# Second layers in another order of tiles, difference parts and raw second-layer weights at other steps

## The chip, the cores and the metric

The kernel runs on one core of one Trainium2 chip. Its time is the device time of the whole program in microseconds (us). A trace of one execution is told in its own time, from the first instruction on (the span).

## What is computed

Two parts follow each other. The first is a gated linear recurrence over 768 positions, for 4 sequences and 8 heads of width 48. The second sends its output, 3072 rows of 384, through four experts, each of two layers with a ReLU between, and adds the results weighted by a probability.

```python
# recurrence: q, k, v, alpha are (4, 8, 768, 48)
for t in range(S):
    state = alpha[:, :, t, :, None] * state + np.einsum('bhd,bhe->bhde', k[:, :, t], v[:, :, t])
    y[:, :, t] = np.einsum('bhd,bhde->bhe', q[:, :, t], state)
x = y.transpose(0, 2, 1, 3).reshape(B * S, H * D)          # (3072, 384)
# experts: w1 is (4, 384, 1024), w2 is (4, 1024, 384)
p = domain_probs / (domain_probs.sum(-1, keepdims=True) + 1e-09)
for e in range(E):
    h = np.maximum(x @ w1[e], 0.0)
    out += p[:, e:e + 1] * (h @ w2[e])
```

## The kernel before

**Blocks, groups, tasks.** The 3072 rows are 24 blocks of 128 positions of one sequence. `attention(u)` computes block `u` of the recurrence: it turns a, k and q into the layout it needs, multiplies decays into q and k over seven levels, takes products on PE, and yields some 17 times on the way. Blocks are gathered in groups: group 0 has two, groups 1 to 5 four each, group 6 two. A *task*, written (g,e) here, is one group with one expert: the first layer ("up"), then the second ("down"). Tasks run in the order (0,0) to (4,3), then (5,0), (6,0), (5,1), (6,1) and so on. The recurrence of later groups is woven into the tasks of earlier ones: `deal` gives each yield of each block a due time by a fixed table (`BEATS`, `IN_PAIRS`), and `advance`, called after each up tile and at each down step, runs what is due. So the program text is one hand-made order; each engine then runs its own instructions in that order, and semaphores make it wait for the others. Five engines take part: PE (matmuls), DVE and ACT (elementwise work), POOL and SP (here mainly issuing transfers).

**Three parts.** From group 1 on matmuls take 32-bit data in a faster, less exact form. To keep the result exact each operand is split in three: a rounded part ("top"), a remainder ("low") and a combination ("difference", scaled by 4096). Weights are split once, written to DRAM (`kept`), and loaded in split form afterwards. A layer is then three matmuls instead of one: parts 0, 1 and 2.

**Up.** `up(gi, e, fc)` makes tile `fc` (0 to 7) of the hidden layer: 9 matmuls (L775) into the PSUM tile `one`, then ACT's ReLU with rounding (L777) into part 0 of `hidden`. One tile later DVE makes the low part from `one` and part 0 (`hidden_rest`, L800), and puts the tile on the list `later`. The difference (`make_dif`, L805) is made during the down. `hidden[c]` holds tiles 2c and 2c+1; the four tiles `hidden[0]` to `hidden[3]` are made anew for each task from a pool `hT` of four buffers.

**Down.** `down` goes through steps (slot, part, fc), a slot being a block of the group: 96 steps for four slots and 48 for two, a matmul each (L847) into the PSUM tile of the slot (`ops`). `one` and `ops` share four PSUM buffers in turn, so the `ops` of the first and second slot take the buffers of the `one` of tiles 4 and 5, and the next up's first tiles take those of the four slots. After the last step of a slot `add_up` scales its sum and adds it to `acc` (L875 on DVE; L873 on ACT for the first expert). Before the change the order is: parts 0 and 1 of the first two slots, parts 0 and 1 of the next two, each over all eight tiles, then part 2 slot by slot. A difference is made at every seventh step, from step 6. In the last down of a group `split_x` splits the next group's x at given steps (L271 and L805 on `xT`).

**Raw second-layer weights.** In group 1 and in (2,0) (`fresh`) the second-layer weights are not in DRAM in split form yet. `load_piece(1, i)` loads them raw (L237, SP's queue), four pieces of 384 KB a task, into a fifth tile of the pool `hT`. Being the next in turn, this takes the buffer of the old task's `hidden[0]`, and later, as the pool goes on in turn, it is `hidden[3]` of the new task that takes this buffer. `split_piece` splits a piece: ACT makes the top (L250), one tile later DVE the two others (L252, L253), and POOL writes them to `kept` (L256). `BESIDE` says at which up tile which piece is queued: `{2: 0, 3: 1, 4: 2, 5: 3}`. `background` starts a queued piece and goes on with those begun. Loads of split weights (L214) and of the recurrence's inputs (L188, L192) are in SP's queue too.

**The recurrence from block 10 on.** Its inputs come in another layout, and DVE transposes them (`turn`, L488). After the transpose of a ACT scales it by a mask (L492), in the same step of `attention`; k follows in the next step, and q, which is multiplied by a (L518), in the one after. Further lines named later: copies of q into `qb` (L541, ACT), the decay multiplied into q and k (L548, L550, L560, DVE), products on PE (L567, L623), scores taken over (L577, DVE), the block's output on PE (L662).

Of the kernel before, what the change touches and what calls it, by code (L numbers as in the profile page):

```python
# [14 lines left out]
ACT = mybir.ActivationFunctionType  # L15
# [5 lines left out]
def kernel(  # L21
# [37 lines left out]
    nc = tc.nc  # L59
# [3 lines left out]
    P = 128  # L63
# [8 lines left out]
    NQ = 4  # L72
    QF = F // NQ
    FPQ = FCH // NQ
    LEVELS = [1 << i for i in range(7)]
    HALF = P // 2
# [8 lines left out]
    n = np.arange(QUAD)[None, :]  # L85
# [13 lines left out]
    ident_all = const.tile([P, P + HALF + 1], F32, name="ident")  # L99
# [18 lines left out]
    LAST = len(groups) - 1  # L118
# [34 lines left out]
    later = deque()  # L153
# [47 lines left out]


    SPLIT_AT = [{1: 2, 4: 3}, {1: 0, 3: 1, 5: 2, 7: 3}]
    BESIDE = [{2: 0, 3: 1, 4: 2, 5: 3}, {1: 2, 2: 3}]

    def load_piece(l, i, beside=False):
        if i >= E * NQ * LAST:
            return
        gi, k = divmod(i, E * NQ)
        e, c = divmod(k, NQ)  # L210
        if gi > l and not (l == 1 and fresh(gi, e)):
            w = wt[l][i] = wts.tile([P, 3, KC * QF], F32R, name=f"w{l + 1}",
                                    bufs=AHEAD if l == 0 else NQ)
            nc.sync.dma_start(out=w.bitcast(F32), in_=kept[l][k])  # L214
            return
        if l == 1 and gi == 0 and not beside:
            return
        if l == 0:

            if e == 0:  # L220
                shared[c] = wts.tile([P, 3, KC * QF], F32R, name="w2", bufs=NQ)
            w = shared[c][:, 2 - e % 2].bitcast(F32)
        else:

            if gi > 1 or gi == 1 and e > 0:
                if c == 0:
                    shared["w2"] = hid.tile([P, NQ, KC * QF], F32, name="hT", bufs=NQ)
                w = shared["w2"][:, c]
            else:
                w = hidden[c][:, gi].rearrange("p f n -> p (f n)")[:, :KC * QF].bitcast(F32)  # L230
        wt[l][i] = w
        if l == 0:
            nc.sync.dma_start(
                out=w.rearrange("p (c f) -> p c f", f=QF),
                in_=moe_w1[e].rearrange("(c p) f -> p c f", p=P)[:, :, c * QF:(c + 1) * QF])
        else:
            nc.sync.dma_start(  # L237
                out=w.rearrange("p (c d) -> p c d", d=DM),
                in_=moe_w2[e].rearrange("(c p) d -> p c d", p=P)[:, c * FPQ:(c + 1) * FPQ])

    def split_piece(l, i):
        gi, k = divmod(i, E * NQ)
        whole = wt[l][i]
        if i >= E * NQ:
            w = wt[l][i] = wts.tile([P, 3, KC * QF], F32R, name="w2", bufs=NQ)
        else:
            w = wts.tile([P, 3, KC * QF], F32R, name="w1", bufs=AHEAD)
        top, both, rest = (w[:, part] for part in range(3))

        nc.scalar.activation(out=top, in_=whole, func=ACT.Copy, scale=LIFT)  # L250
        yield
        nc.vector.tensor_sub(rest, whole, top.bitcast(F32))  # L252
        nc.vector.scalar_tensor_tensor(out=both, in0=rest.bitcast(F32), scalar=4096.0, in1=whole,  # L253
                                       op0=ALU.mult, op1=ALU.add)
        if (gi, k // NQ) != (1, 0):
            nc.gpsimd.dma_start(out=kept[l][k], in_=w.bitcast(F32))  # L256

    def background():


        for piece in list(splitting):
            if next(piece, splitting) is splitting:
                splitting.remove(piece)
        if making and len(splitting) < 4:
            splitting.append(making.popleft())
            next(splitting[-1])
# [17 lines left out]
    def turned(src):  # L284
        tp = ps.tile([P, NP, P], F32, name="tp", tag="w")
        for p in range(NP):
            nc.tensor.transpose(tp[:, p, :], src(p), ident)  # L287
        return tp
# [187 lines left out]
    def attention(u):  # L476
        cb, b = units[u]
        ra, rk, rq, rv = (raw(u, nm) for nm in ("a", "k", "q", "v"))
        pair = lambda t: lambda p: t[:, 2 * p:2 * p + 2, :].rearrange("p b c -> p (b c)")
        keys = lambda: work.tile([P, NP, P], F32, name="KT", bufs=5)  # L480

        AT = work.tile([P, NP, P], F32, name="AT")
        QT = work.tile([P, NP, P], F32, name="QT")

        def turn(nm, out):
            t = runs_of[nm]
            t = bass.AP(tensor=t.tensor, offset=t.offset, ap=[list(t.ap[0]), [RUN, NP], [D, NTOK], [1, QUAD]])
            nc.vector.transpose(out=out.rearrange("p a (t n) -> p a n t", n=NTOK), in_=t)  # L488

        if u >= in_runs:  # L490
            turn("a", AT)
            nc.scalar.activation(out=AT, in_=AT, func=ACT.Copy, scale=ident_all[:, P + HALF:])  # L492
        else:
            nc.scalar.copy(out=AT, in_=turned(pair(ra)))
        after = u + 1 if u > 1 else len(units)
# [1 line left out]
        yield  # L497
        KT = keys()
        if u >= in_runs:
            turn("k", KT)  # L500
        else:
            nc.scalar.copy(out=KT, in_=turned(pair(rk)))
# [130 lines left out]
        parts = lat.rearrange("p (r s i) c -> p r s i c", s=2, i=2)  # L633
# [105 lines left out]
    def up(gi, e, fc, slots=None):  # L739
# [8 lines left out]
        if gi == fc == 0 and begins:  # L748
            for k in range(NQ):
                load_piece(1, e * NQ + k, beside=True)  # L750
        beside = BESIDE[(gi, e) == (1, 0)]
        if fresh(gi, e) and fc in beside:
# [51 lines left out]
    def make_dif(top, low, dif):  # L804
        nc.vector.scalar_tensor_tensor(out=dif, in0=low.bitcast(F32), scalar=-4096.0,  # L805
                                       in1=top.bitcast(F32), op0=ALU.mult, op1=ALU.add)

    def down(gi, e, slots, between):


        first = first_piece(gi, e)
        tiles = range(FCH)
        if gi == 0 and e < E - 1 and slots[0] == (e == 0):
            making.extend(split_piece(0, first + NQ + k) for k in range(2))
        if gi == 0 and e == E - 1 and slots[0] == 1:
            making.extend(split_piece(1, first + NQ + k) for k in range(NQ // 2))
        while fresh(gi, e) and (making or splitting):
            background()

        if gi == 0:  # L820
            steps = [(slot, 3, fc) for slot in slots for fc in tiles]
        else:
            pairs = [slots[k:k + 2] for k in range(0, len(slots), 2)]
            steps = [(slot, part, fc) for parts in ((0, 1), (2,)) for pair in pairs
                     for part in parts for slot in pair for fc in tiles]
        begins = {step[0]: n for n, step in reversed([*enumerate(steps)])}
        ends = {step[0]: n for n, step in enumerate(steps)}
        sums = {}
        for n, (slot, part, fc) in enumerate(steps):
            c, f = divmod(fc, FPQ)  # L830
            advance(cost(1, gi, e) * len(slots) / len(steps))
            while between and n >= between[0][0] * len(steps):
                between.popleft()[1]()
            if n and n % (len(steps) // (2 * len(slots))) == 0:
                background()
            if later and n % (len(steps) // 12 - 1) == len(steps) // 12 - 2:
                make_dif(*later.popleft())
            if n == begins[slot]:
                sums[slot] = ps.tile([P, DM], F32, name="ops", tag="g", bufs=4)
            h = hidden[c][:, :, f, slot * P:(slot + 1) * P]  # L840
            if part < 3:
                w = wt[1][first + c].rearrange("p t (c d) -> p t c d", d=DM)[:, part, f]
                h = h[:, part]
            else:
                w = wt[1][first + c].rearrange("p (c d) -> p c d", d=DM)[:, f]
                h = h[:, 2].bitcast(F32)
            nc.tensor.matmul(sums[slot], lhsT=h, rhs=w, start=(n == begins[slot]), stop=(n == ends[slot]))  # L847
            if n == ends[slot]:
                add_up(gi, e, slot, sums.pop(slot))
        while between:  # L850
            between.popleft()[1]()
        background()
        if slots[-1] == len(groups[gi]) - 1 and gi != LAST - 1:
            for c in range(NQ):
                del wt[1][first + c]
                if gi == 0:
                    continue
                if c < NQ // 2 or gi in (1, LAST):
                    load_piece(1, first + NQ + c)
                else:  # L860
                    late.append(first + NQ + c)
# [27 lines left out]
    def cost(layer, gi, e):  # L889
        n = len(groups[gi]) / 4  # L890
        if layer == 0:
            return 2.1 * n if gi > 0 else 2.6 * n
        return 4.1 if gi > 0 else 5.4
# [50 lines left out]
    def advance(spent):  # L944
        nonlocal clock
        clock += spent
        while waiting and clock >= waiting[0][0]:
            next(waiting.popleft()[2], None)
# [96 lines left out]
```

## Time and profile before

| | |
|---|---|
| time, three runs | 1030.1, 1033.85, 1035.3 us (median 1033.85) |
| the profiled execution, its own time | 1027.61 us |
| its span | 1025.7 us |
| mean granted PE clock | 0.998 |
| HBM traffic | 216 MB read, 42 MB written, 252 GB/s over the span |

The largest groups of instructions, with their busy time and the mean of one:

| line, engine, what | count | busy us | mean ns |
|---|---|---|---|
| L847 PE, second layer from group 1 on | 2112 | 381.8 | 339 |
| L775 PE, first layer, four blocks | 1440 | 342.8 | 394 |
| L541 ACT, copies of q | 322 | 131.1 | 407 |
| L800 DVE, low parts of hT | 192 | 122.3 | 645 |
| L805 DVE, differences of hT | 192 | 112.8 | 640 |
| L777 ACT, ReLU | 192 | 107.9 | 562 |

Matmuls overlap, so the mean of one is longer than the distance from one to the next. A line of a timeline gives the start and the length in us, the engine, the line of the kernel, what is written and read, how many instructions are merged, and in brackets how long the engine sat idle before and what released it. A line of the waits names who waited, for whom, the sum in us, how often, and the longest.

### The profile page before, as it was taken

To read this page: it belongs to the slowest core of one execution; us is meant where nothing else is said; L and a number is where in the kernel's file an instruction comes from. 1 tells how busy PE (TensorE), PEld (TensorE's weight loads), DVE (VectorE), ACT (ScalarE), POOL (GpSimd) and SP (SyncE) were. 2 spreads that over 40 slices of the span, in tenths; PEclk is the share of its full clock that TensorE was granted. 3 is DMA by queue.
4 is the path that set the end of the run, shared out by engine and by line. 5 is a ranking of instruction groups with operands and counts; after the bars stand their busy time and mean duration, and the time that the engine had idled before them with its cause. 6 is when DMAs were issued, how large, how long until landed. Compare 5 with 4: busy or idle time off the path is not lost.

```text
span 1025.7 us, 21120 instructions
## 1 busy us (share of the span) xinstructions
PE 998.4 (97%) x8564; PEld 886.7 (86%) x8564; DVE 702.4 (68%) x1430; ACT 438.7 (43%) x961; POOL 36.1 (4%) x79
## 2 busy tenths in 40 slices
PE   8889999999999999999999999999999999999998
PEld 7667777988888799898898898888988989898998
DVE  5698879687979868677767666885877743434343
ACT  5687666365354444335443415444454332211111
POOL 2010000000000100000000000000000000000000
PEclk9999999999999999999999999999999999999999
DMA  9499699398988999789889759786796454454531
GB/s 214 135 387 282 201 359 338 107 337 265 322 284 249 317 296 330 284 253 317 287 259 334 235 214 385 263 274 261 212 365 250 170 205 184 185 195 174 221 149 47
DMA packets 155632, 260.19 MB, mean 254 GB/s; under 512 B 95216, under 2 KB 132464, under 8 KB 133520
## 3 DMA queue, kind: packets, MB, share of 16 engines
q1 hardware_dynamic: 149072, 216.44, 63.7%
q0 software_dynamic: 6016, 42.08, 10.2%
q8 instruction: 68, 1.11, 0.4%
q10 hardware_dynamic: 448, 0.33, 0.1%
q14 instruction: 28, 0.23, 0.1%
HBM read 216.35 MB, written 42.47 MB: 252 GB/s over the span
## 4 chain that ended last, share of the span: by engine, by line
PE 81%; DVE 11%; ACT 4%; issue 2%; DMA 0%; POOL 0%; DVEq 0%; SPq 0%; ACTq 0%; POOLq 0%
PE ops L847 35%; PE one L775 31%; PE sc L567 5%; PE yps L662 3%; PE one L769 2%; PE tp L287 2%; DVE w L252 2%; ACT qb L541 2%; DVE hT L805 1%; DVE hT L800 1%; DVE near L577 1%; DVE QT L548 1%; PE sps L697 1%; DVE w L253 1%; PE far L623 1%
## 5 line engine op out<-in xcount | busy, mean ns | idle before, releaser
L847 PE MATMUL ops<-w,hT 128*128 128x384 f32 x2112 | 381.8, 339 | 9.4 <-ACT hT L777 6.7
L847 PEld LDWEIGHTS ops<-w,hT 128*128 128x128 f32 x2112 | 366.4, 189 | 15.6 <-ACT hT L777 8.9
L775 PE MATMUL one<-xT,w 128*128 128x512 f32 x1440 | 342.8, 394 | 0.8 <-DVE acc L875 0.8
L775 PEld LDWEIGHTS one<-xT,w 128*128 128x128 f32 x1440 | 266.8, 188 | 58.3 <-DVE acc L875 1.2
L777 ACT ACTIVATE hT<-one 128x512 fp32r<-128x512 f32 (+1 forms) x192 | 107.9, 562 | 343.4 <-PE one L775 318.7
L800 DVE SCALAR_TENSOR_TENSOR hT<-one,hT 128x512 fp32r<-128x512 f32 (+1 forms) x192 | 122.3, 645 | 105.2 <-ACT hT L777 104.8
L541 ACT COPY qb<-QT 64x256 f32<-64x256 f32 x322 | 131.1, 407 | 88.7 <-DVE QT L518 44.9
L548 DVE TENSOR_TENSOR QT<-QT,AT 128x256 f32<-128x256 f32 x158 | 66.7, 422 | 85.9 <-ACT qb L541 85.1
L805 DVE SCALAR_TENSOR_TENSOR hT<-hT 128x512 fp32r<-128x512 f32 (+1 forms) x192 | 112.8, 640 | 0.1
L577 DVE COPY_PREDICATED near<-masks,sc 128x256 f32<-128x256 uint8 x138 | 73.9, 536 | 41.5 <-PE sc L567 38.1
L567 PEld LDWEIGHTS sc<-qb,KT 128*64 128x64 f32 x2208 | 69.7, 138 | 7.3 <-issue 5.7
L567 PE MATMUL sc<-qb,KT 128*64 128x64 f32 x2208 | 74.0, 223 | 0.9 <-ACT qb L541 0.9
L875 DVE SCALAR_TENSOR_TENSOR acc<-ops,p_all,acc 128x384 f32<-128x384 f32 x66 | 40.0, 614 | 42.8 <-PE ops L847 42.8
L560 DVE TENSOR_TENSOR KT<-KT,AT 128x256 f32<-128x256 f32 x161 | 67.4, 418 | 0.0
L559 ACT COPY KT<-KT 128x256 f32<-128x256 f32 x138 | 57.5, 416 | 3.3
L769 PE MATMUL one<-xT,w 128*128 128x256 f32 (+1 forms) x240 | 46.2, 340 | 0.4 <-ACT xT L460 0.4
L847 PE MATMUL ops<-hT 128*128 128x384 f32 x128 | 46.2, 494 | 0.0
L550 DVE TENSOR_TENSOR AT<-AT 128x256 f32<-128x256 f32 (+1 forms) x138 | 39.1, 284 | 4.7
L769 PEld LDWEIGHTS one<-xT,w 128*128 128x128 f32 x240 | 37.7, 191 | 4.9 <-ACT xT L460 0.6
L884 POOL DMA_DIRECT2D out_dram<-acc x22 | 11.9, 540 | 673.7 <-DVE acc L875 673.7
L662 PE MATMUL yps<-lat,rv 128*32 128x128 f32 x736 | 33.1, 273 | 1.6 <-ACT lat L640 1.6
L775 PE MATMUL one<-KT,w 128*128 128x256 f32 x288 | 34.6, 279 | 0.0
(119 smaller groups left out, 709.1 us busy)
## 6 DMA issues: line engine op xcount, KB each, us to landing
w<-kept SPq DMA_DIRECT2D x140, 1152.0 KB, 8.8
kept<-w POOLq DMA_DIRECT2D x32, 1152.0 KB, 8.7
hT<-in_moe_w_dram SPq DMA_DIRECT2D x36, 384.0 KB, 5.9
w<-in_moe_w_dram SPq DMA_DIRECT2D x16, 384.0 KB, 5.8
rv<-in_v_dram SPq DMA_DIRECT2D x24, 192.0 KB, 9.3
out_dram<-acc POOLq DMA_DIRECT2D x22, 192.0 KB, 6.4
rk<-in_k_dram SPq DMA_DIRECT2D x14, 192.0 KB, 6.1
rq<-in_q_dram SPq DMA_DIRECT2D x14, 192.0 KB, 3.0
```

The lines of the kernel that those rows point to most:

```text
L541: nc.scalar.copy(out=qb[rows, :, i, :].rearrange("p a (b r) -> p a b r", r=m), in_=qv[rows])
L548: nc.vector.tensor_mul(qv, qv, spread(dv[:, :, :, 0], m))
L560: nc.vector.tensor_mul(new[:, :, :, 0, :], old[:, :, :, 0, :], spread(halved(decs[li])[:, :, :, 1], m))
L567: nc.tensor.matmul(out[HALF * s:HALF * (s + 1), 2 * p:2 * p + 2, :], lhsT=KTs[li][:, p, HALF * s:HALF * (s + 1)], rhs=qbs[li][:, p, :, QUA ...
L577: nc.vector.copy_predicated(near.rearrange("p a (b two r) -> p a b two r", two=2, r=m)[:, :, :, 1, :], mk.unsqueeze(1).broadcast_to([P, H, ...
L662: nc.tensor.matmul(yps[QUAD * j:QUAD * (j + 1), c, :], lhsT=lhsT, rhs=rhs, start=begins, stop=ends)
L769: nc.tensor.matmul(one, lhsT=w[:, kc], rhs=xraws[gi][:, kc, lo:hi], start=(kc == 0), stop=(kc == KC - 1))
L775: nc.tensor.matmul(one, lhsT=w[:, part, kc], rhs=x_part(gi, part, kc), start=(part == 1 and kc == 0), stop=(part == 0 and kc == KC - 1))
L777: nc.scalar.activation(out=parts[0], in_=one, func=ACT.Relu, scale=TRIM)
L800: nc.vector.scalar_tensor_tensor(out=low, in0=x, scalar=0.0, in1=top.bitcast(F32), op0=ALU.max, op1=ALU.subtract)
L805: nc.vector.scalar_tensor_tensor(out=dif, in0=low.bitcast(F32), scalar=-4096.0, in1=top.bitcast(F32), op0=ALU.mult, op1=ALU.add)
L847: nc.tensor.matmul(sums[slot], lhsT=h, rhs=w, start=(n == begins[slot]), stop=(n == ends[slot]))
```

## The change

Five things move; no computation is added or left out.

1. In the downs from group 1 on, the first two parts of a pair of slots go over tiles 0 to 5 first, and then over tiles 6 and 7. In group 1 part 2 goes over tiles 0 and 1 of all slots first, and then over the other six, slot by slot.
2. A difference is made at every fifth step of a down with four slots, from step 4.
3. In group 1 the raw second-layer weights of the next task are loaded at the step at which part 2 has left tiles 0 and 1 behind, not after the last step.
4. Outside (1,0) each raw piece is queued for its split one up tile earlier.
5. From block 10 on, the scaling of a stands in the step of k's transpose, ahead of it, not in the step of its own.

```diff
     SPLIT_AT = [{1: 2, 4: 3}, {1: 0, 3: 1, 5: 2, 7: 3}]
-    BESIDE = [{2: 0, 3: 1, 4: 2, 5: 3}, {1: 2, 2: 3}]
+    BESIDE = [{1: 0, 2: 1, 3: 2, 4: 3}, {1: 2, 2: 3}]
...
         if u >= in_runs:
             turn("a", AT)
-            nc.scalar.activation(out=AT, in_=AT, func=ACT.Copy, scale=ident_all[:, P + HALF:])
         else:
             nc.scalar.copy(out=AT, in_=turned(pair(ra)))
...
         KT = keys()
         if u >= in_runs:
+            nc.scalar.activation(out=AT, in_=AT, func=ACT.Copy, scale=ident_all[:, P + HALF:])
             turn("k", KT)
...
             pairs = [slots[k:k + 2] for k in range(0, len(slots), 2)]
-            steps = [(slot, part, fc) for parts in ((0, 1), (2,)) for pair in pairs
-                     for part in parts for slot in pair for fc in tiles]
+            steps = [(slot, part, fc) for pair in pairs for some in (tiles[:-FPQ], tiles[-FPQ:])
+                     for part in (0, 1) for slot in pair for fc in some]
+            split = FPQ if gi == 1 else 0
+            steps += [(slot, 2, fc) for some in (tiles[:split], tiles[split:]) for slot in slots for fc in some]
...
-            if later and n % (len(steps) // 12 - 1) == len(steps) // 12 - 2:
+            if later and n % (len(steps) // 24 + 1) == len(steps) // 24:
                 make_dif(*later.popleft())
+            if gi == 1 and (slot, part, fc) == (slots[0], 2, FPQ):
+                for c in range(NQ):
+                    load_piece(1, first + NQ + c)
...
                 if gi == 0:
                     continue
-                if c < NQ // 2 or gi in (1, LAST):
+                if gi == 1:
+                    continue
+                if c < NQ // 2 or gi == LAST:
                     load_piece(1, first + NQ + c)
```

`FPQ` is 2, `NQ` is 4, `LAST` is 6.

## The prediction

> **What bounds the kernel now.** A task is one group and one expert, written (g,e): eight first-layer tiles ("up", 72 matmuls), then the second layer ("down", 96 steps for four blocks, 48 for two). First I read the page's engine table and the windows by stage:
>
> ```profile
> PE 998.4 (97%) x8564; PEld 886.7 (86%) x8564; DVE 702.4 (68%) x1430; ACT 438.7 (43%) x961; POOL 36.1 (4%) x79
> 245.00:290.00 45.00, 42.45 (x347) 36.91 (x346) 36.48 (x69) 21.03 (x44) 2.12 (x4) 1.00 0.86 290
> 290.00:335.00 45.00, 42.62 (x353) 37.61 (x353) 40.49 (x76) 22.72 (x48) 3.21 (x6) 0.96 0.86 283
> 420.00:460.00 40.00, 40.00 (x370) 36.13 (x366) 28.47 (x58) 16.36 (x36) 0.00 (x0) 1.00 0.85 283
> ```
>
> (Columns: length, then busy time of PE, weight load, DVE, ACT, POOL; granted clock; DMA.) From 420 to 460 PE never rests, so nothing can be won there. The second group, 160 to 332 us, has holes in PE, and DVE busy up to 90%. Next the timeline of PE around the starts of the downs, and the chain for the undisturbed pace:
>
> ```profile
> 838.70 16.64 PE ops L847 x96
> ...
> 265.62 1.38 PE L847 MATMUL ops<-w,hT 128*128 128x384 f32 x7
> 281.69 0.44 PE L847 MATMUL ops<-w,hT 128*128 128x384 f32 x1 [0.50 <-DVE hT L805]
> 283.43 4.61 PE L847 MATMUL ops<-w,hT 128*128 128x384 f32 x25 [1.30 <-DVE hT L805]
> ...
> 309.79 1.21 PE L847 MATMUL ops<-w,hT 128*128 128x384 f32 x6
> 312.28 0.44 PE L847 MATMUL ops<-w,hT 128*128 128x384 f32 x1 [1.28 <-ACT hT L777]
> 313.81 7.89 PE L847 MATMUL ops<-w,hT 128*128 128x384 f32 x36 [1.10 <-ACT hT L777]
> ...
> 358.58 0.44 PE L847 MATMUL ops<-w,hT 128*128 128x384 f32 x1 [1.73 <-ACT hT L777]
> ...
> 654.87 4.59 PE L775 MATMUL one<-xT,w 128*128 128x512 f32 x18 [0.85 <-DVE acc L875]
> ```
>
> A step lasts 16.64/96 = 0.1733 us, so six steps from 309.79 end at 310.83; the seventh starts at 312.28 (1.45 lost) and the eighth at 313.81 (1.36 more): tiles 6 and 7 came late. Start-to-start distances above the pace, summed alike from 160 us on: (1,1) 0.28; (1,2) 3.57, of it 2.23 before 281.69 and 283.43 for differences (L805); (1,3) 2.81; (2,0) 2.97; (3,3) 1.56; (4,0) 1.78. That is 12.97 us, all the change can remove but the half clock below. Why tiles 6 and 7 are late, by the waits of ACT:
>
> ```profile
> ACT hT L777 <- DVE w L253: 23.5, 5, 7.0
> ACT AT L492 <- DVE AT L488: 17.6, 7, 4.4
> ```
>
> The raw w2 lies in the buffer that holds tiles 6 and 7 of the next hT; the ReLU (L777) of tile 6 waits until DVE (L253) has split the last raw piece. In the third group and later, ACT instead stands in its queue before AT's scaling (L492), with the ReLU of tile 7 behind it.
>
> **The change part by part.**
>
> *Tiles 6 and 7 later.* No matmul is added. They are wanted at step 24 instead of 6: 18 x 0.1733 = 3.1 us later, and their low parts (L800) at step 28 instead of 22. There are more changes of accumulator; the last phase changes it every 8 steps and still makes 96 in 16.64, so a change costs nothing. The second block's accumulator now begins at step 6, not 8, 0.35 us sooner, and takes the PSUM buffer of tile 5, whose reader is L800(5). The upper end of that cost is in (2,0), below.
>
> *Split a tile sooner, raw load sooner.* Four DVE pairs (0.95 + 0.96) a task move one tile ahead; their sum stays. In SP's queue the raw loads pass one load of q, in (1,0), and nothing elsewhere; they wait for step 71 instead of 89: 3.1 us sooner. That load of q goes from 196.81 to about 200 us, and its transposes on PE start at 234.99. POOL's writes of split pieces keep their order and go a tile sooner. They land 3.0 to 7.7 us after issue, and ACT never waited for them in this group, so the load itself gains 0; it covers the earlier split, which would else move into the landing.
>
> *Differences sooner* (each fifth step instead of each seventh): the last is queued at step 39 instead of 55. It was late in (1,2), at the end of DVE's queue. Attention's DVE work queued in between falls back by up to three differences, 3 x 0.64 = 1.9 us.
>
> *AT's scaling a beat later:* DVE's transpose is done when ACT gets there. Instructions stay.
>
> Now by task, because DVE takes over where PE no longer waits.
> - (1,1): 0.28 won.
> - (1,2): DVE runs without rest from 266.45 to 285.04, when acc of block 0 is done, but for 0.39 before a qb copy, which L492 had delayed. The next up's first tile takes that block's PSUM. PE alone would get there at 284.1 (3.8 sooner); DVE allows 285.04 - 0.39 = 284.65, so 284.7 for 287.88: 3.2 won.
> - (1,3): DVE's order at the end:
>
> ```profile
> 331.40 0.61 DVE L875 SCALAR_TENSOR_TENSOR acc<-ops,p_all,acc 128x384 f32<-128x384 f32 x1
> 331.93 0.68 DVE L271 TENSOR_TENSOR xT<-x_raw,xT 128x512 fp32r<-128x512 f32 x1
> 332.65 0.69 DVE L805 SCALAR_TENSOR_TENSOR xT<-xT 128x512 fp32r<-128x512 f32 x1
> 333.26 0.61 DVE L875 SCALAR_TENSOR_TENSOR acc<-ops,p_all,acc 128x384 f32<-128x384 f32 x1
> ```
>
> In the second group the third part now takes tiles 0 and 1 of all blocks first, so block 0 ends at step 77, not 71. The x split of step 75 (1.33 us from 331.93 to 333.26) then stands ahead of acc. DVE had rested 0.85, 0.38 and 0.75 us since 294; the earlier split fills these. Acc ends at 332.01 - 1.98 + 1.33 = 331.36, and PE follows at 331.4 instead of 332.46: 1.05 won of 2.81. PE waits there some 3.3 us (332.46 - 2.81 - 1.6 for the half clock = 328.05).
> - (2,0): ACT's first raw copy (0.84) now precedes a qb copy that DVE awaits. L800(5) ended 0.03 after the down's start; it has one split pair more ahead (1.86), plus 0.84, less 0.38 of rest filled: 2.3 us, against step 6 at 1.04. A new wait of 1.2 for 2.97: 1.75 won. Its bounds are 0 and 2.3.
> - (3,3): the 0.55 for a difference goes, but acc is bound by DVE; only 0.39 before a qb copy is won: 0.4.
> - (4,0): L492 no longer stands before the ReLU: 1.78, less 0.1 for step 6 in (4,1), where L800(5) ended at 1.02 against 1.04.
>
> Sum: 0.28 + 3.2 + 1.05 + 1.75 + 0.4 + 1.7 = 8.4 us.
>
> The clock drops in one place:
>
> ```profile
> 310.00:313.40 3.40, 1.43 (x7) 0.86 (x5) 3.00 (x4) 1.44 (x3) 0.53 (x1) 1.00 0.96 358
> 313.40:316.80 3.40, 2.99 (x9) 2.99 (x10) 2.96 (x6) 3.35 (x9) 0.00 (x0) 0.51 1.05 408
> 355.00:360.00 5.00, 2.47 (x12) 1.78 (x11) 4.38 (x7) 2.04 (x4) 0.53 (x1) 1.00 0.98 382
> ```
>
> After 3.4 us with PE 42% busy it was half for 3.4 us (36 steps took 7.83, not 6.24: 1.6 lost, hidden since DVE bounds that end); a stretch at 49% kept it. The new wait of 3.3 us at the end of (1,3) is nearer the first row, so I count a drop there: 1.7 in (2,0)'s up, which hides the 1.2 at step 6. Net 0.5, between 0 and 1.7. Sum: 7.9 us.
>
> The Trainium skill, "TensorE: Matmul & The Clock Gate", Part 1, has the half rate come after at least one idle window of about 3.4 us. The trace does not agree: seven matmuls ran in the stretch before the drop. By that rule a wait of 3.3 us brings no drop, and the sum would be 8.4 and the time 1025.4.
>
> **The rivals.**
> 1. *Every wait falls.* PE sets all ends, if DVE's lag is smaller than worked out: 12.97 + 1.6 = 14.6, so 1019.3. For it: PE is 97% busy. Against: DVE's unbroken rows up to 285.04 and 332.01. Chance 0.15.
> 2. *DVE gives nothing back in the second group.* DVE had 40.49 of 45 us there; if the rests are only moved, (1,2), (1,3) and (2,0) win nothing and 0.28 + 0.4 + 1.7 = 2.4 is left: 1031.5. Against: three of the rests are behind waits that go. Chance 0.2.
> 3. *Slower:* the earlier differences push attention's DVE work back 1.9 us, and PE, which takes its queue in order, stops before the products (L567, L623). In the 16 tasks with attention, (1,0) to (4,3), 16 x 1.93 = 30.9, less 7.9: 1056.9. It decides from 7.9/1.93, some four tasks, on. Against: PE waited for qb at L567 only 0.9 us in all, and in the third and fourth groups these products stand at step 63, behind the last difference in both orders. Chance 0.07.
>
> **How the numbers follow.** The profiled execution took 1027.61 (span 1025.7 and 1.9 around it), 6.2 below the median 1033.85. Taken off its own span, 7.9 gives 1017.8, or 1019.7 with the rest; off the median, 1026.0. The forecast has 0.5, with its own range 1023.5 to 1028.5; 0.08 is left for runs that scatter between (those shown span 5.2 us). The range 1018.5 to 1032 takes in rivals 1 and 2. About 0.5% (5.2 us) can be told from no change, that is below 1028.7: 0.47 of the forecast, rival 1, and some of the rest and of rival 2 make faster 0.72; the rest of rival 2 makes same 0.2; slower 0.08.
>
> **What would show it.** Right: no wait on L777 at the starts of the downs, ACT's 23.5 us behind L253 much shorter, no L805 wait in (1,2), L492 without its 17.6 us; instead a wait on acc (L875 before) at the ends of (1,2) and (1,3), and one of about 1 us at step 6 in (2,0). Wrong: PE without waits in the second group (rival 1), or waits before L567, L623 or L662 that were not there (rival 3).

## The result, and the profile after

The changed kernel took 1022.05 us (median of four executions, 1021.24 to 1022.74), the kernel before 1032.3 us beside it. The ratio is 0.9903, with a 95% interval from 0.9884 to 0.9921: 10.2 us gained. The forecast was 1026.0 and 7.9 us, with a range from 1018.5 to 1032.

The two traces have spans of 1025.7 and 1020.8 us, only 4.9 apart, and this has to be sorted out first. Up to the first matmul of (1,0) the two programs do the same in the same order, yet that matmul starts at 158.76 us before and at 161.43 after. From there to the end, called the *tail* from here on, it is 866.98 and 859.36 us: 7.6 us gained. The following lines of the changed kernel's trace answer to those of the prediction: the page's PE line, windows over (1,2), (1,3) and (2,0) (columns as before), and lines of the waits.

```profile
PE 998.8 (98%) x8564; PEld 888.5 (87%) x8564; DVE 701.0 (69%) x1430; ACT 438.5 (43%) x961; POOL 36.1 (4%) x79
...
247.00:288.00 41.00, 40.82 (x342) 36.09 (x341) 34.53 (x66) 20.25 (x44) 2.12 (x4) 1.00 0.89 302
288.00:330.00 42.00, 39.61 (x338) 35.27 (x336) 39.91 (x76) 23.02 (x48) 2.13 (x4) 1.00 0.98 317
330.00:377.00 47.00, 45.83 (x472) 40.25 (x472) 37.40 (x72) 21.75 (x45) 4.29 (x8) 0.97 0.90 295
```

```profile
ACT hT L777 <- DVE w L253: 15.9, 4, 4.5
...
ACT AT L499 <- DVE AT L488: 3.9, 4, 1.8
...
PE one L775 <- DVE acc L882: 3.6, 2, 2.5
```

(L852 and L882 are the old L847 and L875; L499 is the old L492. In the experiments below these numbers shift by a few lines.) DVE is busy for 39.91 of 42 us in (1,3), and PE's waits have another name: no wait for a ReLU is left on PE, but it waits for `acc`. The timeline of PE shows where:

```profile
309.08 7.62 PE L852 MATMUL ops<-w,hT 128*128 128x384 f32 x43
318.15 9.46 PE L852 MATMUL ops<-w,hT 128*128 128x384 f32 x53
330.15 3.65 PE L775 MATMUL one<-xT,w 128*128 128x512 f32 x9 [2.54 <-DVE acc L882]
...
356.98 5.30 PE L852 MATMUL ops<-w,hT 128*128 128x384 f32 x29 [1.03 <-DVE hT L800]
...
651.93 4.34 PE L775 MATMUL one<-xT,w 128*128 128x512 f32 x17 [1.10 <-DVE acc L882]
```

The down of (1,3) starts at 309.08 and runs 43 matmuls without a stop, where before it stopped after six. Its end, 327.6, is followed by a hole up to 330.15 until DVE has made `acc` of block 0. Then nine matmuls take 3.65 us instead of 2.3: the clock is at half. In (2,0) the seventh step waits 1.2 us for a low part.

A task's length is the time from its first up matmul to that of the next task (us):

| task | before | after | forecast gain | measured gain |
|---|---|---|---|---|
| (1,1) | 41.76 | 41.36 | 0.28 | 0.40 |
| (1,2) | 43.96 | 40.91 | 3.2 | 3.05 |
| (1,3) | 44.58 | 43.07 | 1.05 | 1.51 |
| (2,0) | 47.25 | 47.03 | 1.75, less 0.5 for the clock | 0.22 |
| (3,3) | 41.47 | 41.06 | 0.4 | 0.41 |
| (4,0) and (4,1) | 86.35 | 84.33 | 1.7 | 2.02 |

All other tasks from (1,0) on are equal to 0.02 us. The sum is 7.6.

### The profile page after: what moved, and what is told of

Its sections match the earlier page's. It is cut to its first block, busy times and chain, and to the rows that moved or that the text cites. A ratio compares the mean times of both kernels' runs of the same rounds, so it can differ in the third digit from the quotient of the medians.

```text
span 1020.8 us, 21134 instructions
## 1 busy us (share of the span) xinstructions
PE 998.8 (98%) x8564; PEld 888.5 (87%) x8564; DVE 701.0 (69%) x1430; ACT 438.5 (43%) x961; POOL 36.1 (4%) x79
## 3 DMA queue, kind: packets, MB, share of 16 engines
q0 software_dynamic: 6016, 42.08, 10.2%
q8 instruction: 68, 1.11, 0.4%
## 4 chain that ended last, share of the span: by engine, by line
PE 83%; DVE 11%; ACT 3%; issue 2%; DMA 0%; SPq 0%; DVEq 0%; ACTq 0%
PE ops L852 35%; PE one L775 32%; PE sc L567 5%; PE yps L662 3%; PE one L769 2%; PE tp L287 2%; DVE w L252 1%; ACT qb L541 1%; DVE hT L800 1%; PE sps L697 1%; DVE QT L548 1%; DVE near L577 1%; DVE w L253 1%; PE far L623 1%; DVE hT L805 1%
## 5 line engine op out<-in xcount | busy, mean ns | idle before, releaser
L852 PE MATMUL ops<-w,hT 128*128 128x384 f32 x2112 | 377.8, 338 | 1.2 <-DVE hT L800 1.2
L852 PEld LDWEIGHTS ops<-w,hT 128*128 128x128 f32 x2112 | 365.2, 188 | 4.5 <-DVE hT L800 2.0
L800 DVE SCALAR_TENSOR_TENSOR hT<-one,hT 128x512 fp32r<-128x512 f32 (+1 forms) x192 | 122.0, 644 | 101.9 <-ACT hT L777 101.6
L541 ACT COPY qb<-QT 64x256 f32<-64x256 f32 x322 | 131.2, 407 | 98.3 <-DVE QT L518 45.0
L567 PEld LDWEIGHTS sc<-qb,KT 128*64 128x64 f32 x2208 | 69.7, 138 | 7.9 <-issue 6.3
L567 PE MATMUL sc<-qb,KT 128*64 128x64 f32 x2208 | 74.0, 223 | 1.5 <-ACT qb L541 0.8
L882 DVE SCALAR_TENSOR_TENSOR acc<-ops,p_all,acc 128x384 f32<-128x384 f32 x66 | 39.7, 614 | 42.2 <-PE ops L852 42.2
L852 PE MATMUL ops<-hT 128*128 128x384 f32 x128 | 46.2, 494 | 0.0
```

The source lines that it names most:

```text
L541: nc.scalar.copy(out=qb[rows, :, i, :].rearrange("p a (b r) -> p a b r", r=m), in_=qv[rows])
L567: nc.tensor.matmul(out[HALF * s:HALF * (s + 1), 2 * p:2 * p + 2, :], lhsT=KTs[li][:, p, HALF * s:HALF * (s + 1)], rhs=qbs[li][:, p, :, QUA ...
L800: nc.vector.scalar_tensor_tensor(out=low, in0=x, scalar=0.0, in1=top.bitcast(F32), op0=ALU.max, op1=ALU.subtract)
```

## The experiments

All times are medians; each ratio is to the kernel before, run beside it. Waits, task lengths and tails are read from one trace of each run; the waits in the two traces of the kernel before agree to 0.01 us. By the ratios alone, only three of the altered versions lie apart from the changed kernel's 0.9884 to 0.9921: the old differences, the old scaling, and tiles and split both at their old places. For the others the traces decide.

**The kernel before once more** (no edit).

> The kernel before, unchanged, to see how far its executions differ. In the two traces at hand the tail, from the first matmul of (1,0) to the end, is 866.9 us before and 859.4 after: 7.5 us, while the times differ by 10.2. Theory A (the gain is the waits of PE that fell away, 7 to 8 us, and the rest is half-clock stretches, each about 1.5 us, of which the timed executions of before had two or three more than its profiled one): time 1030 to 1034, mean granted clock of the timed executions down to 0.993 to 0.997, spans longer where the clock is lower. Theory B (the waits themselves are longer in the executions without a trace of their own): the clock stays at 0.998 and the spans are longer all the same.

Measured: 1032.85 us over twelve executions, 1028.68 to 1036.73, ratio 1.0 [0.9986, 1.0015]. Its trace has a span of 1029.3 and three stretches at half clock (at 16.7, 286.4 and 317.1 us) where the first trace had one. PE's waits in it are those of the first trace to 0.01 us, and its tail of 868.77 is longer by 1.8, of which 1.55 lie in (1,2) with its half clock. Over the 49 executions of the kernel before that the experiments list with their clock, the mean span is 1030.6 and the mean clock 0.9931; the four of the changed kernel have 1020.1 and 0.9965. A half clock of 3.41 us takes 3.41 x 0.5/1027 = 0.0017 off the clock, so that is about four against two in an execution. A straight line through the 49 gives 655 us of span for a whole unit of clock, or 1.1 us for each half clock; at a clock of 0.9965 the kernel before would have 1028.3. So of 10.4 us between the means some 8.2 are there at equal clock, and some 2.2 come with the clock. Theory A holds: the clock of the twelve lies between 0.987 and 0.996, a little lower than expected, and the spans are longer where it is lower. Theory B's sign, a clock that stays at 0.998, did not come.

**Tiles 6 and 7 at their old steps.**

```diff
-            steps = [(slot, part, fc) for pair in pairs for some in (tiles[:-FPQ], tiles[-FPQ:])
-                     for part in (0, 1) for slot in pair for fc in some]
+            steps = [(slot, part, fc) for pair in pairs for part in (0, 1) for slot in pair for fc in tiles]
```

> The changed kernel with tiles 6 and 7 in their old place (steps 6 and 7); all else as changed. Theory A (the earlier split already lets the ReLU of tile 6 go, so the later tiles are a second cover for the same wait): ReLU of tile 7 ends 0.8 us after the start of most downs, and step 7 is at 1.2, so only (1,2) waits, 0.5 to 1.5 us, and that is hidden by the wait for acc at its end; the wait at the accumulator of the second slot in (2,0) shrinks by 0.35. Tail within 1.5 us of the changed kernel's 859.4. Theory C (the later tiles are the main gain, since they ended the ReLU waits of 7.9 us in the trace of before): tail 865 to 867.

Measured: 1023.89 us, ratio 0.9909 [0.9892, 0.9925]; tail 860.3, 0.9 longer than with the change. The waits are 0.71 us at step 7 of (1,2), 0.76 behind it, and in (2,0) 0.82 at the second slot instead of 1.19, as theory A has it. Theory C falls: the part that moves the tile which PE was seen to wait for is worth 0.9 us once the rest is there.

**The split at its old tile.**

```diff
-    BESIDE = [{1: 0, 2: 1, 3: 2, 4: 3}, {1: 2, 2: 3}]
+    BESIDE = [{2: 0, 3: 1, 4: 2, 5: 3}, {1: 2, 2: 3}]
```

> The changed kernel with each raw piece split at its old tile; all else as changed. Theory A: ReLU of tile 7 ends up to 4.0 us after the start of the down, just ahead of step 24 at 4.16, so no wait there; the wait at step 6 of (2,0) (1.2 us) goes, since one split pair less stands before the low part of tile 5; in exchange DVE's rests in (1,3) are not filled and the wait for acc at its end grows by about 1.2. Tail within 1 us of 859.4. Theory D (the earlier split is what ended the ReLU waits): tail 4 us longer or more, with ACT's ReLU of tile 6 named as releaser of PE.

Measured: 1025.31 us, ratio 0.993 [0.9916, 0.9945]; tail 861.67, 2.3 longer, where at most 1 was expected. As expected no wait for a ReLU came back, and the one at step 6 of (2,0) went. The trace of PE shows the end of (1,3):

```profile
325.76 2.25 PE L852 MATMUL ops<-w,hT 128*128 128x384 f32 x12
331.90 4.21 PE L775 MATMUL one<-xT,w 128*128 128x512 f32 x9 [3.89 <-DVE acc L882]
```

The wait for `acc` is 4.06 us start to start, for 2.70 with the change: the 1.2 expected, and 0.2 more. It comes from rests of DVE in (1,3), which the changed kernel does not have:

```profile
294.85 0.69 DVE L800 SCALAR_TENSOR_TENSOR hT<-one,hT 128x512 fp32r<-128x512 f32 x1 [0.85 <-ACT hT L777]
301.29 1.51 DVE L577 COPY_PREDICATED near<-masks,sc 128x256 f32<-128x256 uint8 x2 [0.39 <-PE sc L567]
```

Not expected were three waits on differences in (2,0), 0.39, 0.43 and 0.43, in place of the one at step 6. Nor was the clock: behind the longer wait it is at half for 6.83 us from 330.00, two stretches and not one. The up of (2,0) takes 25.51 us, with the change 24.60, and 23.29 where the clock is full (in the run with matmuls that fill the wait, below). So some 0.9 of the 2.3 us is clock, and 1.4 the wait. While tiles 6 and 7 stand at their new steps, what the earlier split gives is work for DVE's rests: PE waits for no ReLU with it or without it.

**Both at their old places.** (Both edits above.)

> The changed kernel with both undone: tiles 6 and 7 at steps 6 and 7, and the split at its old tile. Theory A (the two cover the same wait, and only without both it comes back): waits on the ReLU at the starts of the downs of (1,2), (1,3), (2,0), 0.6, 2.1 to 2.8 and 2.3 to 3.0 us; that of (1,3) is hidden by DVE at its end, and the wait at step 6 of (2,0) is replaced. Tail 2 to 4 us longer than 859.4. If the two simply add up, it is longer by the sum of what the single ones show.

Measured: 1027.54 us, ratio 0.9942 [0.9924, 0.9961]; tail 861.43 without a half clock in it, where the changed kernel's 859.36 has one. The ReLU waits are back:

```profile
309.47 1.20 PE L851 MATMUL ops<-w,hT 128*128 128x384 f32 x6
311.95 7.00 PE L851 MATMUL ops<-w,hT 128*128 128x384 f32 x37 [1.28 <-ACT hT L777]
...
332.04 2.35 PE L775 MATMUL one<-xT,w 128*128 128x512 f32 x9 [2.17 <-DVE acc L881]
```

In (1,3) the ReLU wait (1.44 start to start) and a shorter one for `acc` (2.34) stand where the run with the old split has a single one of 4.06: the former is paid out of the latter. To compare the tails, take the half clocks out by the length of the up of (2,0): 23.29 here, as at full clock, 24.60 with the change, 24.83 with the old tiles, 25.51 with the old split. At full clock the tail is then 858.05 with the change, and it is longer by 0.7 with the old tiles, 1.4 with the old split, and 3.4 with both. So the two singles (2.1) do not add up to it. The 1.3 us that are missing stand in (1,1), 0.39 longer, and (2,0), 0.89 longer than at full clock with the change; in both tasks a wait on the ReLU (0.3 and 1.9) is there only when both parts are undone. There the two cover the same wait, and together they are worth those 1.3 us. In (1,2) and (1,3) their effects add up, and the ReLU wait of (1,3) is worth nothing, since DVE sets the end.

**A difference at every seventh step again.**

```diff
-            if later and n % (len(steps) // 24 + 1) == len(steps) // 24:
+            if later and n % (len(steps) // 12 - 1) == len(steps) // 12 - 2:
```

> The changed kernel with a difference made at every seventh step again; all else as changed. Theory A (the last difference, queued at step 55, lands behind attention's work on DVE): waits on L805 come back where DVE lags, 1 to 2 us each in (1,2), (2,0) and (4,0), none in the tasks from (2,1) to (3,2); in (1,3) and (3,3) the wait for acc hides it. Tail 3 to 5 us longer than the changed kernel's 859.4. Rival (the third part's new order, tiles 0 and 1 of all blocks first, already gives the differences the time they need): tail within 1 us, with a wait left in (2,0) and (4,0) only.

Measured: 1025.67 us, ratio 0.9939 [0.9925, 0.9953]; tail 862.23, 2.9 longer, with no half clock in it. The trace of PE in (1,2):

```profile
284.20 1.14 PE L852 MATMUL ops<-w,hT 128*128 128x384 f32 x5 [0.77 <-DVE hT L805]
285.94 3.57 PE L852 MATMUL ops<-w,hT 128*128 128x384 f32 x19 [0.61 <-DVE hT L805]
```

Waits on differences, start to start, are 1.71 in (1,2), 0.79 in (1,3), 1.11 in (2,0) and 0.97 in (4,0), none from (2,1) to (3,2). That is theory A; with the half clock that the changed kernel has and this trace has not, the loss is 4.2 us, the largest of the single parts.

**AT scaled right after its transpose again.**

```diff
             turn("a", AT)
+            nc.scalar.activation(out=AT, in_=AT, func=ACT.Copy, scale=ident_all[:, P + HALF:])
...
-            nc.scalar.activation(out=AT, in_=AT, func=ACT.Copy, scale=ident_all[:, P + HALF:])
             turn("k", KT)
```

> The changed kernel with AT scaled right after its transpose again; all else as changed. Theory A (with tiles 6 and 7 wanted at step 24, the ReLU that stands behind the scaling has 3.1 us more, so the move matters only through DVE's rest of 0.39 us in (1,2) and (3,3)): tail 0 to 1 us longer, no wait on a ReLU. Theory E (the move is what ended the 1.55 us wait of (4,0)): that wait comes back, tail 1.5 us longer.

Measured: 1027.25 us, ratio 0.9951 [0.9935, 0.9966]; tail 862.29, 2.9 longer. Both theories miss: the ReLU wait of (4,0) does not come back, yet the loss is three times the upper end of theory A. The timelines of ACT and DVE at the start of the down of (1,3) show it:

```profile
309.16 0.72 ACT L492 ACTIVATE AT<-AT,ident 128x512 f32<-128x512 f32 x1 [2.46 <-DVE AT L488]
309.79 0.58 ACT L777 ACTIVATE hT<-one 128x512 fp32r<-128x512 f32 x1
...
310.40 0.69 DVE L800 SCALAR_TENSOR_TENSOR hT<-one,hT 128x512 fp32r<-128x512 f32 x1 [0.75 <-ACT hT L777]
```

ACT stands 2.46 us before the scaling, the ReLU of tile 7 is late behind it, and DVE, whose next instruction is the low part of that tile, rests for 0.75 us. PE does not notice here, but at the end of the task: the wait for `acc` is 3.69 instead of 2.70. In (2,0) and (4,0) waits of 0.81 and 0.82 on differences follow. About 0.3 of the 2.9 us is clock: the half clock falls whole into the up of (2,0), which takes 24.86 us for 24.60. In the changed kernel DVE has no rest between 305 and 331 us.

**Part 2 slot by slot, raw load at the end of the down.**

```diff
-            split = FPQ if gi == 1 else 0
-            steps += [(slot, 2, fc) for some in (tiles[:split], tiles[split:]) for slot in slots for fc in some]
+            steps += [(slot, 2, fc) for slot in slots for fc in tiles]
...
-            if gi == 1 and (slot, part, fc) == (slots[0], 2, FPQ):
-                for c in range(NQ):
-                    load_piece(1, first + NQ + c)
...
-                if gi == 1:
-                    continue
-                if c < NQ // 2 or gi == LAST:
+                if c < NQ // 2 or gi in (1, LAST):
```

> The changed kernel with part 2 of the second group slot by slot again and the raw w2 loaded at the end of the down; all else as changed. Theory A (in (1,3) the x split of step 75 stands ahead of acc only because of the new order; the sooner load hides nothing, since it was never awaited): the wait for acc at the end of (1,3) shrinks from 2.7 to about 1.4 us, and without a long wait the half clock after it may go as well; ACT waits for no raw piece. Tail 1 to 3 us shorter than 859.4. Theory F (the earlier split needs the sooner load): ACT waits for the raw pieces at L250, 1 us or more a task in the second group, and the tail is longer. Theory G (the differences need the new order): waits on L805 in (1,2) and (1,3), tail longer by 1 to 2.

Measured: 1020.11 us, ratio 0.9887 [0.9869, 0.9906]; tail 856.96, 2.4 shorter than with the change. DVE at the end of (1,3), and PE behind it:

```profile
327.38 0.61 DVE L876 SCALAR_TENSOR_TENSOR acc<-ops,p_all,acc 128x384 f32<-128x384 f32 x1
327.91 0.68 DVE L271 TENSOR_TENSOR xT<-x_raw,xT 128x512 fp32r<-128x512 f32 x1
328.63 0.69 DVE L805 SCALAR_TENSOR_TENSOR xT<-xT 128x512 fp32r<-128x512 f32 x1
```

```profile
328.05 2.52 PE L775 MATMUL one<-xT,w 128*128 128x512 f32 x9 [1.20 <-DVE acc L876]
```

`acc` stands ahead of the last x split again, the wait is 1.36 us start to start, and the nine matmuls behind it take 2.52 us at full clock. (1,3) takes 41.74 instead of 43.07, (2,0) 45.91 instead of 47.03. So of the 2.4 us, 1.3 are the half clock that does not come, and 1.1 the shorter wait. This part of the change costs more than it gives; theories F and G fall.

**The raw load at its old place, part 2 in the new order.** (Of the edit above, the two parts on `load_piece`.)

> The changed kernel with the raw w2 of the second group loaded at the end of the down again, but part 2 in its new order. Theory A (no one waits for the raw pieces, so the sooner load gains nothing): tail within 0.5 us of 859.4 apart from a half clock more or less (1.4 us), and ACT waits for no raw piece in the second group. Theory F (the earlier split needs it): ACT waits at L250 for the landing, 1 us or more a task.

Measured: 1023.99 us (four executions, clocks 0.993 to 0.995), ratio 0.9921 [0.9905, 0.9938]; tail 859.54 against 859.36, with the same waits to 0.1 us and a half clock at the same place. ACT waits for no raw piece after 170 us. So the sooner load gains nothing. The time is 1.9 us longer all the same. In the trace 1.8 us of it lie ahead of (1,0), whose first matmul starts at 163.24, where the two programs do the same; of the other three executions only the lower clock is known.

**Matmuls that fill the wait.**

```diff
                 down(gi, e, slots, between)
+            if (gi, e) == (1, E - 1):
+                spin = ps.tile([P, NP, P], F32, name="spin", tag="w")
+                for _ in range(9):
+                    nc.tensor.matmul(spin[:, 0], lhsT=ident, rhs=ident, start=True, stop=True)
```

> The changed kernel with nine matmuls of 128 columns, whose result nobody reads, put on PE at the end of (1,3), in the wait for acc of 2.7 us (about 0.21 us each, 1.9 us together). Theory A (the half clock after that wait comes from PE being busy for less than about 0.43 of a stretch of 3.41 us of the clock's own grid; in ten traces so far every such stretch later than 20 us was followed by half clock, and of those above only one): the stretch is busy for 0.7 or more, no half clock near 330 us, (2,0) takes 45.9 us instead of 47.0, and the tail is 1 to 1.5 us shorter than 859.4. The time is 1 us shorter. Rival (the clock falls for another reason, such as the work that follows): the half clock stays, and the tail is 859 to 860.

Measured: 1022.43 us, ratio 0.9907 [0.989, 0.9924]; tail 858.05, 1.3 shorter. The windows of the changed kernel, and then of this one, on the grid on which the clock changes:

```profile
326.20:329.60 3.40, 1.41 (x9) 1.09 (x7) 3.30 (x8) 1.57 (x4) 0.00 (x0) 1.00 0.97 238
329.60:333.00 3.40, 2.85 (x7) 2.27 (x8) 3.22 (x7) 0.00 (x0) 2.04 (x4) 0.50 1.03 378
```

```profile
327.20:330.60 3.40, 2.89 (x24) 2.70 (x22) 3.33 (x7) 1.05 (x3) 0.00 (x0) 1.00 1.01 318
330.60:334.00 3.40, 3.38 (x47) 2.73 (x49) 3.07 (x7) 0.93 (x2) 2.15 (x4) 1.00 0.82 306
```

PE busy for 1.41 of 3.40 us is followed by a clock of 0.50, 2.89 by 1.00. (2,0) takes 45.69 instead of 47.03, so this half clock cost 1.3 us. The wait at step 6 of (2,0) is 1.19 in both: the low part of tile 5 (L800) ends 2.18 us after the start of the down with the half clock and without it. The shorter time that was expected does not show: the median is 1022.43, for 1022.05 with the change, and the five executions scatter by 2.3 us.

**Two versions meant to beat both kernels.** The first has the old part 2 and load in (1,3) alone, and in every down the first slot's parts 0 and 1 before the second slot's; the second has the old part 2 and load in the whole second group, and in (2,0) alone tiles 0 and 1 of all blocks first. The edit of the second (beside the two on `load_piece`; the first has `split = FPQ if gi == 1 and e < E - 1 else 0`, and the old load in (1,3) alone):

```diff
-            steps = [(slot, part, fc) for pair in pairs for some in (tiles[:-FPQ], tiles[-FPQ:])
-                     for part in (0, 1) for slot in pair for fc in some]
-            split = FPQ if gi == 1 else 0
+            steps = []
+            for pair in pairs:
+                steps += [(slot, part, fc) for slot in pair for part in (0, 1) for fc in tiles[:-FPQ]]
+                steps += [(slot, part, fc) for part in (0, 1) for slot in pair for fc in tiles[-FPQ:]]
+            split = FPQ if (gi, e) == (2, 0) else 0
```

> A version meant to beat both: the third part in its old order, and the raw load at its old place, in (1,3) alone; and in every down with two or four blocks the first slot's parts 0 and 1 over tiles 0 to 5 before the second slot's, so that the second slot's PSUM buffer is wanted at step 12 and not at 6. Theory A: the wait for acc after (1,3) falls to about 1.4 us, perhaps without a half clock after it; the wait of 1.2 us in (2,0) falls to 0.3 (the low part of tile 5 ends 2.2 us after the start, and is wanted at step 11, 1.9 us). Tail 2 to 3.7 us shorter than 859.4, so 855.7 to 857.4, and the time 1018 to 1020. Rival (the low parts, wanted from step 6 now and not from 12, become the wait in the other tasks): tail the same or longer, with L800 as releaser.

> A version meant to beat all: part 2 slot by slot and the raw load at the end of the down in the whole second group, as in the run with the third part as before (tail 857.0); in (2,0) alone part 2 takes tiles 0 and 1 of all blocks first, since there acc is made on ACT; and the first slot's parts 0 and 1 come before the second slot's, so that the second slot's PSUM buffer is wanted at step 12. Theory A: in (2,0) the wait of 1.2 us at step 6 shrinks to 0.3, and the two waits on differences of 0.43 each, which followed it in the last version, fall as the differences of tiles 2 to 7 are wanted six steps later. (2,0) takes 45.0 us, the tail is 856.1. Rival (DVE's work in (2,0) is the bound, wherever PE waits for it): (2,0) takes 45.8 to 45.9, the tail 857.

Measured: the first 1019.37 us, ratio 0.9876 [0.9861, 0.9892], tail 857.15. The wait at the second slot in (2,0) fell to 0.32, but two waits on differences of 0.43 each took its place, and (2,0) takes 45.85 instead of the 45.91 of the run with the third part as before. Its time and tail are within what was expected, by the shorter wait after (1,3), with no half clock behind it, and not by (2,0). The second 1019.06 us, ratio 0.9872 [0.9854, 0.989], tail 855.88, (2,0) 44.87. The prediction for it (45.0 and 856.1) holds: in (2,0) the order, and not DVE's sum of work, was the bound. Against the changed kernel's 0.9903 it is ahead by some 3 us, though the intervals just overlap (0.9884 to 0.9890); its tail is 3.5 shorter, 1.3 of it the half clock that does not come. Against the run with the third part as before (0.9887) the times do not tell it apart, the tails do by 1.1.

## Why the prediction was right, and where not

- *PE's holes in the second group, (2,0), (3,3) and (4,0) are all there is to win.* Right: no other task from (1,0) on changed its length by more than 0.02 us. That the sum of the tasks, 7.6, is so near the forecast's 7.9 is in part luck: (2,0) gave 1.0 less than forecast, the others together 0.8 more.
- *The end of (1,2) passes to DVE, 3.2 won.* 3.05, with 0.42 of wait for low parts and 0.19 for `acc`.
- *The x split of step 75 stands ahead of acc in (1,3), so only 1.05 of 2.81 are won, and PE waits some 3.3 us.* The mechanism is shown by the run with the third part as before. Mis-sized: 1.51 won and a wait of 2.70.
- *DVE's rests of 0.85, 0.38 and 0.75 us are filled by the earlier split.* The first two are: with the old split 0.85 and 0.39 come back. The last is not: the run with the old scaling brings 0.75 back with the earlier split in place. I had put the scaling's move down at 0.39 us twice and the ReLU of (4,0); it is worth some 3 us of tail.
- *A new wait of 1.2 at step 6 of (2,0).* 1.19. *A half clock behind the wait of (1,3).* It came.
- *The half clock hides the 1.2 at step 6, net 0.5.* This step failed. The half clock cost 1.3 us whole and the wait stayed at 1.19 with and without it. In this up DVE rests 3.7 us for one of ACT's copies (L541) with the half clock and without it, and that copy stands in ACT's queue behind a ReLU that waits for PE. So DVE's chain starts later by as much as the up is slower, and the low part that step 6 waits for ends 2.18 us after the start of the down in both.
- *L800(5) against step 6 in (4,1), 0.1 lost.* Nothing: (4,1) takes 43.52 in both.
- *ACT's 23.5 us behind L253 fall to much less.* Only to 15.9, but no matmul waits for a ReLU behind them any more.
- *The raw load gains 0.* Shown. *The end of block 0 at step 77 costs DVE's order 1.33.* Shown, and with the half clock the whole of that part was a loss of 2.4 us of tail.
- *The median 1026.0.* It is 1022.05, in the whole range but below the forecast's own, 1023.5 to 1028.5. Of the 3.95 us, 1.55 are the starting point: the kernel before had 1032.3 beside the changed one, not the 1033.85 of the three earlier runs. The rest is the gain: the tail gained 7.6 for 7.9, but the time 10.2. I took the working of one execution with a single half clock off the median of executions which, as it turned out, have about four. What was missing is the 2 us that go with two fewer of them, not another wait. Where in the timed executions those half clocks lay is not known, so it is not shown that the change removed them, and not chance.
- Rival 1 did not come: waits of 5.8 us are left. Rival 2 neither: (1,2) kept 3.05. Rival 3 neither: PE's wait for `qb` at L567 is 0.8 us in all, for 0.9.

## What to carry to other kernels

When a wait of the bounding engine falls, follow the order of the next engine up to the point where the first waits for it again; here the ends of three downs were set by DVE's queue, and a change that put 1.33 us ahead of one accumulation cost more than its other half gave. A rest of the second engine is worth looking for even where the first does not wait: the largest surprises, the scaling's move and the earlier split, worked through rests of 0.4 to 0.9 us on DVE. And compare executions from a common point inside the program, with the clock beside them, before you explain a difference of one per cent.

## What the runs showed of the hardware that was not expected

PE's clock falls to half for 3.41 us at a time, on a fixed grid of that length that starts at another point in each execution. In the 13 traces of this study every stretch of that grid later than 20 us in which PE was busy for 0.42 or less of the time, by the records of matmuls, was followed by half clock (23 of them, 7 being the last full stretch of their trace). Of the ten from 0.429 to 0.495 three were (0.431, 0.442, 0.474) and seven were not; from 0.50 on none was. Ahead of 20 us this does not hold: there a stretch at 0.65 was followed by half clock too. So the same wait brings a half clock or not, depending on how it falls on the grid: the waits at the end of (1,2), equal to 0.01 us in the two traces of the kernel before, left PE busy for 0.68 and 0.79 of two stretches in the first, with no half clock behind them, and for 0.47 of one in the second, with a half clock. Much of the scatter of one kernel goes with this: the shortest and the longest of the 49 executions of the kernel before, with clocks of 0.996 and 0.987, are 8.2 us apart, and 655 us for a unit of clock gives 5.9 of them. The Trainium skill, "TensorE: Matmul & The Clock Gate", Part 1, describes a free-running window of 3413 ns, which agrees with the 3.41 us here. It gives an idle window as the condition for the half rate, and the traces differ: 1.41 us of matmuls in the window did not prevent it.
